# Loads of v behind the block moves, and a group's first sum and difference made with its last gate/value piece

## The chip, the cores and the metric

The kernel runs on one core of a Trainium2 chip. The metric is the device time of one execution in microseconds, the median of several runs. The engines named here are TensorE (PE in the profile; PEld is its weight load), VectorE (DVE), ScalarE (ACT), GpSimd (POOL) and SyncE (SP), which computes nothing and issues most of the DMAs. Each engine works through its own list of instructions in order; a semaphore wait of one instruction holds everything behind it on that engine.

## The reference

Two stages follow each other. The first is a linear attention with a decaying state, for 4 batches, 8 heads, 768 positions and head size 48; the second is a gated feed-forward block on the 3072 rows of 384 numbers that the first one leaves.

```python
# attention, for each position t
cur = einsum('bhd,bhe->bhde', u * k[t], v[t])
y[t] = einsum('bhd,bhde->bhe', r[t], state + cur)
state = w * state + einsum('bhd,bhe->bhde', k[t], v[t])
# feed-forward: x is (3072, 384), w_gate and w_val (384, 1536), w_out (1536, 384)
g = x @ w_gate
out = (g * sigmoid(g) * (x @ w_val)) @ w_out
```

## The kernel before

**Attention in blocks.** The 768 positions are cut in 6 chunks of 128, so there are 24 blocks (chunk times batch), numbered 0 to 23. For a block, r and k are scaled by powers of w (`scale_k` L329, `scale_r` L332, both on GpSimd), turned so that the head dimension lies on the partitions, multiplied into scores (L423), masked into `At` (L433, L437), and `outputs` (L476) multiplies `At` with v and the turned r with the state `Z`. `update` (L491, L503, L504) advances the state with k and v. `own_product` (L254, L255) and `own_sum` (L260) make the diagonal term with u.

**The turn of blocks 12 to 23** is made by sixteen small DMAs (`move_blocks`, L386, SyncE's queue), which move 32x32 blocks within `hats`, and two transposes on VectorE (`turn_blocks`, L401: first into `kT`, then into `rT`). Between these two transposes one piece of the feed-forward work is taken from the list of pieces. The moves of block s+1 overwrite what the transposes of block s read, so they wait for VectorE; they also wait for the scaled r and k. Two blocks share a buffer of scaled r, so the scaling of the r of an odd block (the even steps from 12 on, named `late`) waits for the moves of the even block before it.

**Loads.** `load` (L141) brings k and r of a block three steps ahead, `load_v` (L148) brings v one step ahead into one of four buffers; `outputs` and `update` of a block read v two steps after that. From block 12 on each is six DMAs. In the kernel before, step s of the main loop issues, in SyncE's queue: `load_v(s + 1)`, then (not when `late`) `load(s + 3)`, then the moves of s+1, then (when `late`) `load(s + 3)`.

**The feed-forward block** works on groups g of 256 rows (two attention blocks). From g = 2 on, two groups g and g+1 are taken together. Their gate and value products are made by `three_beside` (g = 2, 4, 6, beside the attention) and `three_units` (g = 8, 10, behind it): blocks of 3x3 are multiplied with 15 products instead of 18, from sums of weight blocks (`w_forms`, L700, GpSimd) and of x (L727); L770 are the products, L794 the additions that put them together in `hv`, L801 the sigmoid-gated unit, L794 also its multiplication. The additions, and the multiplication that gives `hT`, are mostly VectorE's; the last multiplication, of group g+1, is kept back in `last`.

**The output product** `project` (L589) uses 7 products instead of 8 on the halves of `hT` and of `w_out`. It needs sums and differences of the quarters of `hT`, which `h_sums` makes on VectorE: with n = 0 the sum L562 and the difference L563, with n = 1 L565 and L566. `two_projections` gives the order of the items "00 10 01 02 11 04 ...": the first digit j picks the group g or g+1, the second the product p. The item "10" starts with `h_sums(g, 0)`, and "02" is the first product that reads its result. The item "01" first does what `last` kept back, then `h_sums(g, 1)`.

**The order of the work** is written out by hand: pieces of the feed-forward block stand in one list, and `gaps` takes a share of them at five places of each step of the main loop. `queue` fills the list: for a pair the other items of the pair before, then the pieces of `three_beside`, then item "00" of this pair, then the last piece. Item "10" comes first when the next pair is queued. The tail behind the loop runs `three_units` and the rest of the projections.

Output stores (L613) go through ScalarE's queue. SyncE's DMAs and these share eight semaphores in turn, so that in the built program each DMA also waits for the one eight places before it.

Of the kernel before, what the change touches and what calls it, by code (L numbers as in the profile page):

```python
# [22 lines left out]
def fast(  # L23
# [102 lines left out]
    def places(i, n):  # L126

        if i < SWAPPED:
            return [(slice(0, P), slice(0, n), 0)]
        return [  # L130
            (slice(0, P), slice(0, n // 2), 0),
            (slice(0, 64), slice(n // 2, n), 64),
            (slice(64, P), slice(n // 2, n), -64),
        ]

    def load(i):
        c, b = divmod(i, B)
        for src, dst in zip((k, r), raw(i)):
            for p, h, o in places(i, H):
                rows = slice(P * c + p.start + o, P * c + p.stop + o)  # L140
                sp.dma_start(out=dst[p, h], in_=src[b, h, rows, :].rearrange("h t d -> t h d"))  # L141

    def load_v(i):
        c, b = divmod(i, B)
        for e in range(2):
            for p, a, o in places(i, HP):
                rows = slice(P * c + p.start + o, P * c + p.stop + o)
                sp.dma_start(  # L148
                    out=v_ld[i % 4][p, a, 64 * e : 64 * e + D],
                    in_=v[b, :, rows, :].rearrange("(a e) t d -> e t a d", e=2)[e][:, a],  # L150
                )
# [99 lines left out]
    def own_product(i):  # L251
        kl, rl = raw(i)
        rk = two.tile([P, H, D], FP32, name="rk", tag="rk")[:]
        pool.tensor_mul(rk, rl, kl)  # L254
        pool.tensor_mul(rk, rk, ub)  # L255
        rks[i] = rk

    def own_sum(i):
        dus[i] = three.tile([P, H], FP32, name="du", tag="du")
        dve.tensor_reduce(dus[i][:], rks.pop(i), axis=AX.X, op=ALU.add)  # L260
# [67 lines left out]
    def scale_k(i):  # L328
        pool.tensor_mul(khat[i % 4][:, :, 0:D], raw(i)[0], kscale)  # L329

    def scale_r(i):
        pool.tensor_mul(rhat_of(i)[:, :, 0:D], raw(i)[1], rscale)  # L332
# [32 lines left out]
    def turn(i):  # L365
        kr = khat[i % 4], rhat_of(i)
        tps = [next_psum(HP, P) for _ in kr]
        turned[i] = three.tile([P, HP, P], FP32, name="rT", tag="rT")
        for tp, t, dst, table in zip(tps, kr, (kT[i % 2], turned[i]), (pw[:, :, 1 : P + 1], pv)):
            for a in range(HP):  # L370
                pe.transpose(tp[:, a, :], pair(t, a), ident[:])  # L371
            if i < 4:
                dve.tensor_mul(dst[:], tp[:], table)
            else:
                act.copy(dst[:], tp[:])

    def move_blocks(i):


        h = hats[:].rearrange("p n h x -> p (n h x)")  # L380
        first, step = ((0, 1), (11, -1), (12, 1), (23, -1))[i % 4]
        for m in range(4):
            for q in range(4):
                src = h[32 * q : 32 * q + 32, P * first + 32 * m : P * first + 32 * m + 1]
                dst = h[32 * m : 32 * m + 32, P * 31 + 32 * q : P * 31 + 32 * q + 1]
                sp.dma_start(  # L386
                    out=bass.AP(
                        tensor=dst.tensor, offset=dst.offset,
                        ap=[list(dst.ap[0]), [-P, 2 * HP], [1, 32]],
                    ),  # L390
                    in_=bass.AP(
                        tensor=src.tensor, offset=src.offset,
                        ap=[list(src.ap[0]), [P * step, 2 * HP], [1, 32]],
                    ),
                )
# [152 lines left out]
    def h_quarters(g):  # L548
        return [
            hT[g][:, FH * k : FH * (k + 1), P * j : P * (j + 1)] for j in range(2) for k in range(2)  # L550
        ]

    def h_sums(g, n):
        h11, h12, h21, h22 = h_quarters(g)
        if g < THREES:
            t = three.tile([P, 2, FH, P], FP32, name="hs", tag="w_bits")
        else:
            t = room["hs"][2 * (g % 2) + n]
        x = part_of.setdefault(g, {})
        x["s"] = x.get("s", ()) + (t[:, 0], t[:, 1])  # L560
        if n == 0:
            dve.tensor_add(t[:, 0], h22, h21)  # L562
            dve.tensor_sub(t[:, 1], t[:, 0], h11)  # L563
        else:
            dve.tensor_sub(t[:, 0], h11, h21)  # L565
            dve.tensor_sub(t[:, 1], h12, x["s"][1])  # L566
# [62 lines left out]
    def two_projections(g):  # L629

        def item(j, p):
            if g >= FIRST and (j, p) == (0, 1):
                for do in wide.pop("last"):
                    do()
            if (j, p) in ((1, 0), (0, 1)):
                h_sums(g, p)
            elif (j, p) in ((1, 1), (0, 3)):
                h_sums(g + 1, p // 3)
            if g + 2 < N // 2:
                prepare_threes(g + 2, order.index(f"{j}{p}"))  # L640
            project(g + j, p)
        order = "00 10 01 02 11 04 03 12 05 06 13 14 15 16".split()
        return [lambda j=int(o[0]), p=int(o[1]): item(j, p) for o in order]


    FIRST, THREES = 2, 8
# [19 lines left out]
    wide, todo_forms, todo_x = {}, deque(), deque()  # L666
# [74 lines left out]
    def prepare_threes(g, n):  # L741
        if n == 6:
            x_forms(g)
        for _ in range(2):
            if todo_x:
                todo_x.popleft()()
        if g > THREES:
            return
        if n == 1:
            if g == FIRST:  # L750
                todo_forms.extend(in_place(0) + in_place(1))
            if g == THREES:
                todo_forms.extend(w_forms(g, 1))
        if n == 7:
            todo_forms.extendleft(reversed(w_forms(g, 0)))
        for _ in range(2):
            if todo_forms:
                todo_forms.popleft()()
# [26 lines left out]
    def three_beside(g):  # L785
# [18 lines left out]
        for t in range(4):  # L804
# [21 lines left out]
            for k in range(6):  # L826
                i, j = divmod(k, 2)
# [44 lines left out]
        steps, last = [], []  # L872
        for at, do in sorted(todo, key=lambda x: x[0]):
# [3 lines left out]
            if at == int(at):  # L877
                steps.append([])
            steps[-1].append(do)
        steps[-1].append(lambda: wide.update(last=last))  # L880
        pieces = [[] for _ in range(26)]
        for n, q in enumerate(steps):
            pieces[n if n < 3 else 3 + (n - 3) * 23 // 57] += q
# [140 lines left out]
    BLOCKS = 12  # L1024
# [85 lines left out]
    for s in range(4, N + 2):  # L1110
        if 4 < s < N:
            own_sum(s)
        late = BLOCKS < s + 1 < N and s % 2 == 0
        if s + 2 == SWAPPED:
            halves_of = two.tile([P, H, D], FP32, name="swapped", tag="rk")[:].rearrange(
                "p (n h) d -> p n h d", n=2
            )
            for p, o in ((slice(0, 64), 64), (slice(64, P), -64)):
                sp.dma_start(
                    out=halves_of[p], in_=scales[p.start + o : p.stop + o, 1:3, H // 2 : H]  # L1120
                )
        if s + 1 == SWAPPED:
            pool.tensor_copy(scales[:, 1:3, H // 2 : H], halves_of)
        if s + 1 < N:
            scale_k(s + 1)
            if not late:
                scale_r(s + 1)
            own_product(s + 1)
            load_v(s + 1)
            if s + 3 < N and not late:  # L1130
                load(s + 3)
        if s < BLOCKS:
            turn(s)
        gaps(s, 0)
        if 4 <= s - 1 < N:
            while small:
                small.popleft()()
            scores(s - 1)
            if s >= LATE:
                outputs(s - 2)  # L1140
                update(s - 2)
            gaps(s, 1)
        if BLOCKS <= s < N:
            turn_blocks(s)
        if late:
            scale_r(s + 1)
        if BLOCKS <= s + 1 < N:
            move_blocks(s + 1)
        if late and s + 3 < N:
            load(s + 3)  # L1150
        gaps(s, 2)
        if s - 2 >= 4 and (s < LATE or s > N):
            outputs(s - 2)
            update(s - 2)
        if s >= 5 and s % 2:
            queue((s - 3) // 2)
        if s < N:
            diagonal(s)
        if s - 2 >= 4:
            gaps(s, 3)  # L1160
        gaps(s, 4)
        if s == 12:

            dve.tensor_tensor(bad, held[:], wcol[:], ALU.not_equal)
            dve.tensor_reduce(badc, bad, axis=AX.X, op=ALU.add)
            dve.memset(ones, 1.0)
            n_ps = next_psum(HP, P)
            pe.matmul(n_ps[0:1, 0, 0:1], badc, ones, start=True, stop=True)
            act.copy(outside, n_ps[0:1, 0, 0:1])
# [426 lines left out]
```

## Time and profile before

| | |
|---|---|
| median of 3 runs | 600.33 us (599.98 to 602.51) |
| the profiled execution | 599.74 us |
| its span, first to last instruction | 598.0 us |
| granted TensorE clock, mean | 0.999 |
| busy: PE, DVE, ACT, POOL | 582.6, 405.0, 228.0, 313.6 us |
| block moves in SyncE's queue | 192 DMAs of 32 KB, median 2.0 us from issue to landing |
| loads of v, last twelve blocks | 24 DMAs of 48 KB and 48 of 24 KB, median 2.2 and 2.1 us |

In the rows of a timeline the first number is the start in microseconds from the span's beginning, the second the time from the first start to the last end of the instructions merged in the row, then come engine, line, operation, what is written and read, the shapes and the number of instructions. In square brackets stands for how long the engine was idle before the row and who released it. In the rows of the waits the three numbers are the total, the count and the longest, in microseconds. SPq is SyncE's queue: its rows last as long as the issue, and the transfer lands later.

### The profile page before, as it was taken

The numbers are of one execution on the slowest core, as the hardware profiler recorded it, in microseconds if no ns is written. First come the engines' busy times: TensorE is split into PE (matmuls) and PEld (weight loads), VectorE is DVE, ScalarE is ACT, GpSimd is POOL, SyncE is SP. The second block draws the span as 40 slices with busy tenths as digits, with TensorE's granted clock in tenths as the row PEclk, the third lists the DMA queues.
The fourth block names the chain that finished last, engine by engine and source line by source line (L and its number), as shares of the span: only waits on it lengthen the run. The fifth ranks groups of instructions, "written<-read, shape, count | busy, mean of one in ns | idle before, by whom it ended". The sixth has DMA issues, their size and how long they took to land.

```text
span 598.0 us, 12924 instructions
## 1 busy us (share of the span) xinstructions
PE 582.6 (97%) x5112; PEld 524.4 (88%) x5112; DVE 405.0 (68%) x682; ACT 228.0 (38%) x524; POOL 313.6 (52%) x352
## 2 busy tenths in 40 slices
PE   8799999999999999999999999899999999999996
PEld 7678888899888889988889988789988899988896
DVE  6877877369478877478778476769356685277650
ACT  3468887331353422254331344332034321233310
POOL 5789889998999402977610996503445100011000
PEclk9999999999999999999999999999999999999999
DMA  7989893232431323133233232300100000000001
GB/s 163 248 226 249 225 299 75 41 61 58 93 57 21 63 38 72 41 62 59 35 59 70 70 61 46 48 2 3 44 9 2 1 1 27 26 2 0 2 1 57
DMA packets 139830, 40.66 MB, mean 68 GB/s; under 512 B 130160, under 2 KB 133616, under 8 KB 139760
## 3 DMA queue, kind: packets, MB, share of 16 engines
q1 hardware_dynamic: 136304, 35.02, 27.3%
q10 hardware_dynamic: 3456, 4.72, 2.2%
q8 instruction: 42, 0.69, 0.5%
q14 instruction: 28, 0.23, 0.1%
HBM read 28.51 MB, written 4.72 MB: 56 GB/s over the span
## 4 chain that ended last, share of the span: by engine, by line
PE 83%; POOL 4%; DVE 3%; SPq 2%; issue 1%; DMA 1%; ACT 1%; POOLq 0%; DVEq 0%
PE bank L770 28%; PE bank L589 26%; PE ring L770 13%; PE bank L514 7%; PE ring L476 5%; PE ring L423 2%; SPq L386 2%; POOL wgv L242 1%; POOL s L700 1%; DVE hv L794 1%; PE ring L491 1%; PE ring L371 1%; DMA r_ld<-in_r_dram 1%; DVE hs L563 1%; POOL hats L332 0%
## 5 line engine op out<-in xcount | busy, mean ns | idle before, releaser
L794 DVE TENSOR_TENSOR hv<-hv,bank 128x512 f32<-128x512 f32 x132 | 88.0, 683 | 29.1 <-PE bank L770 18.7
L514 PE MATMUL bank<-xT,wgv 128*128 128x256 f32 x288 | 66.8, 385 | 0.6 <-ACT xT L480 0.6
L913 POOL TENSOR_TENSOR hv<-At,hats 128x512 f32<-128x512 f32 x8 | 10.2, 1272 | 107.0 <-ACT At L912 107.0
L770 PE MATMUL bank<-xf,wgv 128*128 128x256 f32 x256 | 66.0, 382 | 0.0
L350 ACT ACTIVATE At<-ident,du 128x128 f32<-128x128 f32 x176 | 60.5, 398 | 14.1 <-DVE hv L602 7.5
L794 ACT COPY hv<-bank 128x512 f32<-128x512 f32 x72 | 40.2, 586 | 61.3 <-PE bank L770 55.0
L514 PEld LDWEIGHTS bank<-xT,wgv 128*128 128x128 f32 x288 | 53.2, 190 | 8.9 <-ACT xT L480 0.9
L700 POOL TENSOR_TENSOR s<-wgv 128x256 f32<-128x256 f32 x39 | 30.0, 793 | 53.1 <-PE bank L589 53.0
L770 PEld LDWEIGHTS bank<-xf,wgv 128*128 128x128 f32 x256 | 47.8, 190 | 7.0 <-DVE kT L904 0.6
L589 PE MATMUL bank<-wo,hv 128*128 128x192 f32 x288 | 49.6, 327 | 0.0
L589 PEld LDWEIGHTS bank<-wo,hv 128*128 128x128 f32 x288 | 47.2, 190 | 0.6
L589 PE MATMUL bank<-wt,hs 128*128 128x192 f32 x240 | 42.1, 327 | 1.4 <-DVE hs L563 1.4
L595 ACT COPY hv<-bank 128x192 f32<-128x192 f32 x36 | 11.3, 318 | 83.9 <-PE bank L589 83.9
L589 PE MATMUL bank<-wo,hs 128*128 128x192 f32 x240 | 42.5, 327 | 0.0
L589 PEld LDWEIGHTS bank<-wt,hs 128*128 128x128 f32 x240 | 39.2, 190 | 2.4 <-issue 1.3
L589 PEld LDWEIGHTS bank<-wo,hs 128*128 128x128 f32 x240 | 39.5, 190 | 0.4 <-DVE hv L597 0.3
L801 ACT ACTIVATE hv<-hv 128x512 f32<-128x512 f32 (+1 forms) x33 | 21.1, 667 | 48.3 <-DVE hv L794 48.3
L770 PE MATMUL bank<-xT,s 128*128 128x256 f32 x152 | 35.5, 380 | 1.6 <-POOL s L700 1.6
L476 PE MATMUL ring<-At,v_ld 128*32 128x128 f32 x768 | 34.9, 273 | 1.5 <-DMA v_ld<-in_v_dram 1.5
L770 PE MATMUL bank<-xT,wgv 128*128 128x256 f32 x144 | 35.6, 380 | 0.0
L770 PEld LDWEIGHTS bank<-xT,s 128*128 128x128 f32 x152 | 28.6, 190 | 6.4 <-POOL s L700 2.0
L504 POOL TENSOR_TENSOR Z<-Z,w 48x192 f32<-48x192 f32 x32 | 17.3, 540 | 31.4 <-DVE Z L503 30.2
(190 smaller groups left out, 1296.2 us busy)
## 6 DMA issues: line engine op xcount, KB each, us to landing
hats<-hats SPq DMA_DIRECT2D x192, 32.0 KB, 2.0
w_bits<-in_moe_w_gate_dram SPq DMA_DIRECT2D x6, 768.0 KB, 6.1
w_bits<-in_moe_w_val_dram SPq DMA_DIRECT2D x6, 768.0 KB, 6.4
w_bits<-in_moe_w_out_dram SPq DMA_DIRECT2D x6, 768.0 KB, 7.0
out_dram<-hv ACTq DMA_DIRECT2D x24, 192.0 KB, 1.9
v_ld<-in_v_dram SPq DMA_DIRECT2D x24, 96.0 KB, 5.7
k_ld<-in_k_dram SPq DMA_DIRECT2D x8, 192.0 KB, 3.6
r_ld<-in_r_dram SPq DMA_DIRECT2D x8, 192.0 KB, 4.0
```

What stands on the lines that cost most here:

```text
L350: lambda h=h: act.activation(At[i % 2][:, h, :], ident[:], AF.Identity, scale=du[:, h : h + 1])
L386: sp.dma_start(out=bass.AP(tensor=dst.tensor, offset=dst.offset, ap=[list(dst.ap[0]), [-P, 2 * HP], [1, 32]],), in_=bass.AP(tensor=src.ten ...
L423: pe.matmul(ps[e][keys, a, cols], kT[i % 2][rows, at(i, a), keys], turned[i][rows, at(i, a), cols], start=True, stop=True, skip_group_chec ...
L476: pe.matmul(ps[32 * q : 32 * q + 32, cc, :], *x, start=start, stop=stop, skip_group_check=True,)
L504: pool.tensor_mul(ze, ze, w)
L514: pe.matmul(gv[:, o, :].rearrange("p (i t) -> p i t", i=2), wt[:, c, P * f : P * (f + 1)], xT[:, 2 * g % NX : 2 * g % NX + 2, c, :], start ...
L589: pe.matmul(ps, lhs[:, f, :], rhs[:, f, :], start=(f == 0 and n in (0, 1, 4)), stop=(f == FH - 1), skip_group_check=True,)
L595: act.copy({0: o1[:, 0:NH], 2: o1[:, NH:DM], 3: o2[:, NH:DM]}[n], ps)
L700: op(made[o], made[a], made[b])
L770: pe.matmul(ps[:, o], u[:, o], v, start=first and o == 0, stop=True, skip_group_check=True,)
L794: do(out, *(pair_of(wide[a][:]) if isinstance(a, str) else a for a in args))
L801: todo.append((at, lambda: act.activation(gate, gate, AF.Silu)))
```

## The change

Two edits. The first: for blocks 12 to 23 `load_v` is issued right behind the sixteen moves of the same block; for `late` steps that is still ahead of `load(s + 3)`. Blocks before 12 keep their order. The second: for the groups g = 2, 4 and 6 `h_sums(g, 0)` is no longer the first thing of item "10" of the projections but the last thing of the last piece of `three_beside`. For the others it stays where it was.

```diff
@@ two_projections / item
-            if (j, p) in ((1, 0), (0, 1)):
+            if (j, p) == (0, 1) or (j, p) == (1, 0) and not FIRST <= g < THREES:
                 h_sums(g, p)
             elif (j, p) in ((1, 1), (0, 3)):
                 h_sums(g + 1, p // 3)
@@ three_beside
-        steps[-1].append(lambda: wide.update(last=last))
+        steps[-1] += [lambda: wide.update(last=last), lambda: h_sums(g, 0)]
@@ main loop
             own_product(s + 1)
-            load_v(s + 1)
+            if s + 1 < BLOCKS:
+                load_v(s + 1)
             if s + 3 < N and not late:
                 load(s + 3)
...
         if BLOCKS <= s + 1 < N:
             move_blocks(s + 1)
+            load_v(s + 1)
         if late and s + 3 < N:
             load(s + 3)
```

(`FIRST` is 2, `THREES` is 8, `BLOCKS` is 12, `N` is 24.)

## The prediction

> **What bounds the kernel now.** I read the page first, then who waited for whom on TensorE, then the timelines around those waits, the SyncE queue last.
>
> ```profile
> PE 582.6 (97%) x5112; PEld 524.4 (88%) x5112; DVE 405.0 (68%) x682; ACT 228.0 (38%) x524; POOL 313.6 (52%) x352
> ```
>
> TensorE is busy for 582.6 of 598.0 us. No matmul is added or removed, so only its 15.4 us of idle time can change. By the busy time in stretches, 7.0 of them lie in the first 60 us and 5.4 at the end, where the change does nothing. Between 200 and 420 us TensorE waits four times, 3.0 us in all:
>
> ```profile
> PE bank L770 <- POOL s L700: 1.6, 1, 1.6
> PE bank L589 <- DVE hs L563: 1.4, 3, 0.6
> ```
>
> The second row is what the moved sum and difference (h_sums) feed: three groups, three waits. The first of them, by the timeline:
>
> ```profile
> 216.90 4.06 PE L589 MATMUL bank<-wo,hv 128*128 128x192 f32 x24
> 218.90 0.70 DVE L401 STREAM_TRANSPOSE kT<-hats 128x512 f32<-128x512 f32 x1
> 219.53 0.92 DVE L562 TENSOR_TENSOR hs<-hv 128x768 f32<-128x768 f32 x1
> 219.77 0.30 ACT L595 COPY hv<-bank 128x192 f32<-128x192 f32 x1
> 220.48 0.96 DVE L563 TENSOR_TENSOR hs<-hs,hv 128x768 f32<-128x768 f32 x1
> 221.59 2.19 PE L589 MATMUL bank<-wt,hs 128*128 128x192 f32 x12 [0.62 <-DVE hs L563]
> ```
>
> Only the transpose of kT (L401) stands between the gate/value work on VectorE and the sums. The second:
>
> ```profile
> 307.48 1.28 DVE L794 TENSOR_TENSOR hv<-hv,bank 128x512 f32<-128x512 f32 x2
> 309.61 4.17 PE L589 MATMUL bank<-wo,hv 128*128 128x192 f32 x24
> 310.26 0.74 DVE L437 COPY_PREDICATED At<-mask,ring 128x512 f32<-128x512 int32 x1 [1.50 <-ACT At L350]
> 310.88 0.73 DVE L503 TENSOR_TENSOR Z<-ring,Z 48x192 f32<-48x192 f32 x2
> 311.64 0.97 DVE L562 TENSOR_TENSOR hs<-hv 128x768 f32<-128x768 f32 x1
> 313.94 2.19 PE L589 MATMUL bank<-wt,hs 128*128 128x192 f32 x12 [0.16 <-DVE hs L563]
> ```
>
> VectorE idles 1.5 us in front of the masked copy L437, with the sums queued behind it. The third wait is at 407.68.
>
> The longest wait, at 377.38, is put down to GpSimd by the page. But the built program's waits show that these matmuls need a sum of a set finished at 364.4, and VectorE's addition of the bank. That addition is the first of the three at 376.59; with 0.69 us each it ends at 377.28. It stood behind a transpose that waited for block moves:
>
> ```profile
> 374.48 0.71 DVE L401 STREAM_TRANSPOSE kT<-hats 128x512 f32<-128x512 f32 x1 [1.95 <-DMA hats<-hats]
> 376.59 1.84 DVE L794 TENSOR_TENSOR hv<-hv,bank 128x512 f32<-128x512 f32 x3
> 377.38 1.97 PE L770 MATMUL bank<-xT,s 128*128 128x256 f32 x8 [1.64 <-POOL s L700]
> ```
>
> The block moves' queue, SyncE's:
>
> ```profile
> 340.46 11.71 SPq L386 DMA_DIRECT2D hats<-hats  x16
> ...
> 352.21 1.96 SPq L141 DMA_DIRECT2D k_ld<-in_k_dram  x3
> 354.21 1.90 SPq L141 DMA_DIRECT2D r_ld<-in_r_dram  x3
> 356.22 3.88 SPq L148 DMA_DIRECT2D v_ld<-in_v_dram  x6
> 360.20 12.50 SPq L386 DMA_DIRECT2D hats<-hats  x16
> ```
>
> Write M22 for the moves of block 22, v22 for its load of v, L23 for the loads of k and r. From 340.46 to 372.70 the queue issues without a pause, and the last of M22 lands at 374.1: SyncE's issue time does reach TensorE here, once.
>
> **First part: the sums earlier.** The built order of VectorE differs in two places alone.
> Group 2 (219 us): L562 and L563 go in front of the kT transpose, which delays them from 218.90 to 219.53. They come 0.63 us earlier. Can TensorE use it? 12 matmuls of this kind take 1.95 us (0.1625 each), so the 24 from 216.90 would be followed at 220.80; the sums now release at 221.59-0.63 = 220.96. Still a short wait, so the gain is 0.63. ScalarE's copy of the same bank (L595), which the matmul also needs, ended at 220.07. The kT transpose comes 1.9 us later; its reader is a later score. rT, which releases the next moves, has the same four instructions ahead of it as before: nothing.
> Group 4 (308 us): they go in front of L437 and the two L503, and can start at 308.76, where the pair of L794 ends, in time that VectorE now idles. They end near 310.7 (0.95 each, no GpSimd work beside them then). TensorE's natural place is 309.61+24x0.1625 = 313.51, so the gain is 313.94-313.51 = 0.43, with 2.8 us of cover left; ScalarE's copy of the bank is at 311.87 to 312.19, so it does not bind. L437 slips from 310.26 to about 310.7 and the two L503 with it, some 0.4; behind them wait GpSimd's scaling of Z, which is then idle till 328.19, and outputs that TensorE starts at 330.8. Nothing.
> Group 6: the built order is the same as before (both transposes already stand in front), so its 0.57 us stays.
> Sum: 0.63+0.43 = 1.06 us.
>
> **Second part: the loads of v.** Six DMAs (3.9 to 4.9 us of issue) per block, blocks 12 to 23, move behind the sixteen moves. The queue's end was v20, L22, M20, v21, M21, L23, v22, M22, v23, M23; it becomes L22, M20, v20, M21, v21, L23, M22, v22, M23, v23. So between two runs of moves there is still exactly one load of v, an earlier block's. M21 to M22: before L23 and v22 (3.96+3.98), after v21 and L23. M22 starts at 360.2 both times. VectorE's rT would have let it go at 357.7, but the 2.5 us aren't gained. At the first run, M12, v12 does go away, but L14 in front was held by GpSimd till 118.74 with SyncE idle from 113.7: nothing.
> What does move: L15, L17, L19, L21, L23 are issued 4 us later. The first four are read 7 us or more after they would land (L15: issued till 162.1, read at 174.2). L23 is tight: it would be issued 356.2 to 360.1, and rows of its kind land after 2.5 to 2.9 us, so r is there at about 362.1, where GpSimd's product L254 starts at 361.28 now: 0.8 us late. Behind it stand L255 and one sum of weights, read by TensorE at about 378; GpSimd then has 2.3 us idle in front of 366.73. Hidden.
> v itself comes some 16 to 27 us later: v22 is issued at 372.8 and read at 416.5. Its buffer's readers are two blocks back and done; SyncE's waits on them cost nothing.
> The output stores on ScalarE's queue share semaphores with SyncE's DMAs, each waiting for the one eight back. In the new program two wait for later moves of M20 (the second until about 328.6, where it is issued at 328.48: 0.1 us, on an engine 38% busy), and eight wait for the last moves and v23, landed by 394, the first being due at 422.
> M22 now follows L23 and not v22. The Trainium skill (DMA: Bandwidth & Descriptors, "Queues, rings and completion order") says that each DMA engine consumes descriptors in ring order, which speaks against the change, as L23 moves 384 KB against v22's 192. The rows: k and r land after 2.6 to 2.9 us, v after 2.1. By the rule M22's first moves land up to 0.8 us late; its last is issued 12 us later, when that backlog is gone, so by the rows it lands as now. I take 0; 0.8 stays for the range.
>
> **Does the 1.06 survive to the end?** The stall at 377 closes a loop: TensorE's last L589 (327.9) releases GpSimd at 328.19, which works without a gap till the scaling of r ends at 340.44; that releases M21, then v21, L23, M22, VectorE, TensorE. Its start moves with TensorE, so the stall arrives as much earlier and stays as long. From 416 on TensorE waits for no one. So the profiled execution of 599.74 us (span 598.0) becomes 598.7; the median of the runs, 600.33, lies 0.6 above it and becomes **599.3**.
>
> **Rivals.**
> *The load's move frees M22.* If an issue of v really leaves the stretch M21 to M22, M22 starts 2.4 us earlier and the stall (377.38-375.57 = 1.8) goes: 597.5. For it: the queue has no pause there. Against: the count above.
> *The sums don't reach TensorE*, because something else releases those matmuls: 600.3. Against: the 0.14 us from the end of L563 to the matmul, both times.
> *Slower: M22 lands later.* The loop has no slack at 377, so each us by which its SyncE stretch grows is one on TensorE. M22 already takes 12.50 where M23 takes 10.49; its slow issues (1.26 and 1.54 us against 0.61) coincide with 16 KB packets of the instruction queue at 361.5 and 368.9. Two more such meetings cost 1.9: 601.2. From 1.06 us on this outweighs the gain, and a whole load of v too much in the stretch (4.0) would give 603.3.
>
> **How the numbers follow.** Likeliest 0.68 (598.5 to 600.3: the sums give from 0.63, group 2 alone, to 1.22, both waits wholly gone, with the 0.6 us to either side by which the profiled run and the median differ); freed 0.09; no effect 0.09; slower 0.14. I take half a per cent, 3.0 us, as about what a measurement of this kernel can tell from no change. Below 597.3: half of the freed case and a trace of the likeliest, 0.06. Above 603.3: half of the slower case, 0.07. The rest, 0.87, is within. The range leaves out most of the freed case and the worse half of the slower one: 597.9 to 601.4.
>
> **What the new profile would show.** Right: the waits of L589 for hs gone at group 4 and at about 0.2 in group 2, still 0.6 in group 6; VectorE with both sums before L437 near 308.7; one load of v between every two runs of moves; a wait of 1.6 to 2 us on L770 near 376; L254 of block 23 waiting for r. Wrong: that last wait on L770 gone or doubled, a new wait of TensorE on At or Z, or ScalarE held before a store.

## The result, and the profile after

The changed kernel takes 598.58 us in the median of 22 runs (597.7 to 601.37), the kernel before, run beside it on the same chip, 599.95 us (598.75 to 602.51). That is 1.37 us less in the medians; the ratio is 0.9979, with a 95% interval of 0.9970 to 0.9987, or 0.8 to 1.8 us. The profiled executions give 596.9 against 598.0 us of span, and 598.61 against 599.74 us in all. TensorE has the same work as before; this row of the page is that of after:

```profile
PE 582.5 (98%) x5112; PEld 524.6 (88%) x5112; DVE 404.6 (68%) x682; ACT 228.3 (38%) x524; POOL 313.2 (52%) x352
```

The waits of TensorE between 200 and 420 us, after (total, count, longest, in us):

```profile
PE bank L770 <- POOL s L700: 1.2, 1, 1.2
PE bank L589 <- DVE hs L563: 0.6, 1, 0.6
```

Of the three waits on hs (1.4 us in all) one is left, the one of group 6. The wait on L770 is there still, 0.4 us shorter. Now the timelines of after, all engines, at group 2:

```profile
217.32 4.06 PE L589 MATMUL bank<-wo,hv 128*128 128x192 f32 x24
219.32 0.95 DVE L562 TENSOR_TENSOR hs<-hv 128x768 f32<-128x768 f32 x1
220.31 0.96 DVE L563 TENSOR_TENSOR hs<-hs,hv 128x768 f32<-128x768 f32 x1
221.18 0.70 DVE L401 STREAM_TRANSPOSE kT<-hats 128x512 f32<-128x512 f32 x1
...
221.41 2.19 PE L589 MATMUL bank<-wt,hs 128*128 128x192 f32 x12
```

The transpose stands behind the sums. From the first of the 24 matmuls to the first on hs it is 4.09 us, before 4.69. At group 4:

```profile
308.62 0.95 DVE L562 TENSOR_TENSOR hs<-hv 128x768 f32<-128x768 f32 x1
309.55 4.17 PE L589 MATMUL bank<-wo,hv 128*128 128x192 f32 x24
309.61 0.96 DVE L563 TENSOR_TENSOR hs<-hs,hv 128x768 f32<-128x768 f32 x1
310.48 0.73 DVE L437 COPY_PREDICATED At<-mask,ring 128x512 f32<-128x512 int32 x1
...
313.56 2.11 PE L589 MATMUL bank<-wt,hs 128*128 128x192 f32 x12
```

The sums fill the time in which VectorE had idled in front of L437, and are done 3 us before TensorE reads them. The end of SyncE's queue, after:

```profile
339.78 11.13 SPq L386 DMA_DIRECT2D hats<-hats  x16
351.00 3.95 SPq L148 DMA_DIRECT2D v_ld<-in_v_dram  x6
355.00 1.89 SPq L141 DMA_DIRECT2D k_ld<-in_k_dram  x3
356.93 1.90 SPq L141 DMA_DIRECT2D r_ld<-in_r_dram  x3
358.94 12.67 SPq L386 DMA_DIRECT2D hats<-hats  x16
371.72 3.95 SPq L148 DMA_DIRECT2D v_ld<-in_v_dram  x6
```

Between M21 (339.78) and M22 (358.94) there is one load of v, ahead of L23 now instead of behind it, and the queue has no pause. What follows from it on VectorE and TensorE, after:

```profile
373.36 0.71 DVE L401 STREAM_TRANSPOSE kT<-hats 128x512 f32<-128x512 f32 x1 [1.51 <-DMA hats<-hats]
...
375.48 1.84 DVE L794 TENSOR_TENSOR hv<-hv,bank 128x512 f32<-128x512 f32 x3
...
376.27 1.97 PE L770 MATMUL bank<-xT,s 128*128 128x256 f32 x8 [1.22 <-POOL s L700]
```

It is the same chain as before, from the moves' landing to the transpose, the addition and the matmul. (The sum of GpSimd, to which the row puts the wait down, ends within 0.1 us of that addition and is held by the same landing, so the trace alone doesn't tell the two apart; that it is the addition rests on the waits of the built program.)

**Where the time went.** All kernels here give TensorE the same matmuls in the same order, so the start of each can be set against that of the same matmul before. The difference changes in a few places only, given here by the times of the kernel before. In the changed kernel it is +0.42 us from 60 us on (a slower start, where nothing was changed). It falls by 0.59 at 221.6 us (group 2), of which 0.10 is lost again at 225.7, by 0.40 at 313.9 and 0.22 at 318.0 (group 4), and by 0.42 at 377.4. The sums gave 1.12 us of this, and the 0.42 at 377.4 makes up for the slower start: 1.1 us, as the two spans have it.

### The profile page after: what moved, and what is told of

Its sections match the earlier page's. It is cut to its first block, busy times and chain, and to the rows that moved or that the text cites. A ratio compares the mean times of both kernels' runs of the same rounds, so it can differ in the third digit from the quotient of the medians.

```text
span 596.9 us, 12929 instructions
## 1 busy us (share of the span) xinstructions
PE 582.5 (98%) x5112; PEld 524.6 (88%) x5112; DVE 404.6 (68%) x682; ACT 228.3 (38%) x524; POOL 313.2 (52%) x352
## 4 chain that ended last, share of the span: by engine, by line
PE 85%; POOL 4%; SPq 2%; DVE 1%; issue 1%; DMA 1%; ACT 1%; POOLq 0%
PE bank L770 28%; PE bank L589 27%; PE ring L770 13%; PE bank L514 7%; PE ring L476 5%; PE ring L423 3%; SPq L386 2%; POOL wgv L242 1%; PE ring L491 1%; PE ring L371 1%; POOL hats L332 1%; POOL rk L254 0%; POOL hats L329 0%; POOL rk L255 0%; DMA k_ld<-in_k_dram 0%
## 5 line engine op out<-in xcount | busy, mean ns | idle before, releaser
L794 DVE TENSOR_TENSOR hv<-hv,bank 128x512 f32<-128x512 f32 x132 | 88.0, 684 | 28.9 <-PE bank L770 18.5
L770 PE MATMUL bank<-xf,wgv 128*128 128x256 f32 x256 | 66.0, 382 | 0.0
L794 ACT COPY hv<-bank 128x512 f32<-128x512 f32 x72 | 40.2, 586 | 60.8 <-PE bank L770 54.5
L770 PEld LDWEIGHTS bank<-xf,wgv 128*128 128x128 f32 x256 | 47.8, 190 | 7.0 <-DVE kT L904 0.6
L770 PE MATMUL bank<-xT,s 128*128 128x256 f32 x152 | 35.5, 380 | 1.2 <-POOL s L700 1.2
L770 PE MATMUL bank<-xT,wgv 128*128 128x256 f32 x144 | 35.6, 380 | 0.0
L770 PEld LDWEIGHTS bank<-xT,s 128*128 128x128 f32 x152 | 28.6, 190 | 5.9 <-POOL s L700 1.6
```

Of the source, the lines that this page charges most:

```text
L770: pe.matmul(ps[:, o], u[:, o], v, start=first and o == 0, stop=True, skip_group_check=True,)
L794: do(out, *(pair_of(wide[a][:]) if isinstance(a, str) else a for a in args))
```

## The experiments

Each kernel's time stands beside that of the kernel before on the same chip, since the chips differ; in brackets is the number of executions.

**The sums alone.** Against before:

```diff
-            if (j, p) in ((1, 0), (0, 1)):
+            if (j, p) == (0, 1) or (j, p) == (1, 0) and not FIRST <= g < THREES:
...
-        steps[-1].append(lambda: wide.update(last=last))
+        steps[-1] += [lambda: wide.update(last=last), lambda: h_sums(g, 0)]
```

> Only the second edit: the sums earlier, the loads of v where they were before. Theory A (the sums give the gain, the loads of v nothing): the waits of L589 for hs at groups 2 and 4 shrink as in the changed kernel, M22 starts some 0.7 us before 360.2, and the time is 0.9 to 1.1 us below the kernel before, about 598.9 to 599.1. Rival B (the loads of v give it): within 0.3 us of the kernel before. Rival C (half from each): 0.6 us below.

598.13 us (12 runs) against 599.09 (23): 0.96 less in the medians, ratio 0.9990 (0.9977 to 1.0003). The interval takes in no change; the trace is clearer. TensorE's difference to before falls at the sums as in the changed kernel, in all by 1.12 us, and by 0.54 at 377. M22 starts at 358.30, 1.9 us before 360.20 and not 0.7: M21 took 11.22 us instead of 11.71, and the start of the kernel was 0.3 us faster too. So theory A holds for the sums, and the stall at 377 moves in a way that it doesn't explain.

**The loads alone.** Against before:

```diff
-            load_v(s + 1)
+            if s + 1 < BLOCKS:
+                load_v(s + 1)
...
             move_blocks(s + 1)
+            load_v(s + 1)
```

> Only the first edit: loads of v behind the moves, the sums where they were before. Theory A: the stretch from M21 to M22 still holds one load of v and L23, so M22 starts within 0.6 us of 360.2, TensorE's wait on L770 near 377 stays between 1.2 and 2 us, and the time is that of the kernel before to 0.4 us. Rival B: 1.0 to 1.4 us below the kernel before. Rival D (the later L23 or v costs something that the sums hid): 0.5 us or more above it.

598.21 us (12) against 599.09 (23): 0.88 less, ratio 0.9983 (0.9973 to 0.9994). More than theory A allows. The difference to before falls in one place, at 377.4, by 1.16 us: the wait on L770 is 0.48 us and not 1.64. M22 starts at 359.72, within 0.6 of 360.20 as A has it, but its sixteen issues take 11.98 us and not 12.50.

**The other two orders.** The changed kernel has the loads of v of odd and even blocks behind the moves. In the first of these two the odd blocks' are ahead, in the second the even blocks':

```diff
@@ odd_before
-            if s + 1 < BLOCKS:
+            if s + 1 < BLOCKS or late:
                 load_v(s + 1)
...
             move_blocks(s + 1)
-            load_v(s + 1)
+            if not late:
+                load_v(s + 1)
```

```diff
@@ even_before
-            if s + 1 < BLOCKS:
+            if s + 1 < BLOCKS or not late:
                 load_v(s + 1)
...
             move_blocks(s + 1)
-            load_v(s + 1)
+            if late:
+                load_v(s + 1)
```

> The changed kernel, but the loads of v of the odd blocks from 13 on are ahead of their moves again; those of the even blocks stay behind. The queue's end is M20, v20, v21, M21, L23, M22, v22, v23, M23: no load of v between M21 and M22. Theory A (one load of v in that stretch is what M22 waits for): M22 starts when VectorE's rT lets it, near 357.2 and not 358.94, the kT transpose comes at about 371.9 and not 373.36, the wait of 1.2 us on L770 goes, and the time is 1.2 us below the changed kernel, about 597.4. Rival E (the stall comes from GpSimd, to which the profile puts it down, or from the moves' own landing): the wait stays and the time is the changed kernel's to 0.3 us.

> The changed kernel, but the loads of v of the even blocks are ahead of their moves again; those of the odd blocks stay behind. The queue's end is v20, M20, M21, v21, L23, v22, M22, M23, v23: two loads of v between M21 and M22. Theory A (the stretch has no slack): M22 starts 4.0 us later, near 362.9, the wait on L770 grows from 1.2 to about 5.2 us, and the time is 4.0 us above the changed kernel, about 602.6. Rival F (some of it is taken up, for TensorE has other pieces to do or the moves go faster without a load behind them): 1 to 3 us above. Rival E: the changed kernel's to 0.3 us.

**odd_before**: 596.32 us (6) against 599.09 (23), ratio 0.9949 (0.9934 to 0.9964), the fastest kernel of this study. Its queue, with the moment it idles in front of M22:

```profile
350.46 1.96 SPq L141 DMA_DIRECT2D k_ld<-in_k_dram  x3
352.47 1.90 SPq L141 DMA_DIRECT2D r_ld<-in_r_dram  x3
356.75 12.44 SPq L386 DMA_DIRECT2D hats<-hats  x16
369.31 7.93 SPq L148 DMA_DIRECT2D v_ld<-in_v_dram  x12
```

and the place of the stall on VectorE and TensorE:

```profile
371.42 0.69 DVE L401 STREAM_TRANSPOSE kT<-hats 128x512 f32<-128x512 f32 x1
...
373.69 2.75 PE L770 MATMUL bank<-xT,s 128*128 128x256 f32 x12
```

SyncE is done with L23 at 354.4 and waits 2.4 us for VectorE's rT. The transpose no longer waits for the moves, and the twelve matmuls, which had been 4 and 8 with the stall between them, run through. Rival E, by which the wait stays, falls.

**even_before**: 605.23 us (6) against 599.09 (23), ratio 1.0091 (1.0069 to 1.0114). M22 starts at 364.48, 24.36 us behind M21 instead of 19.16, and the stall grows to 4.46 us. That is 3.2 us more than after, less than the 4.0 of theory A; but the time is 6.1 us above before. The rest is in the clock. The row of the stall in this kernel's timeline, and then its stretches around the stall, with the granted TensorE clock ahead of the last two figures:

```profile
380.14 3.75 PE L770 MATMUL bank<-xT,s 128*128 128x256 f32 x8 [4.46 <-POOL s L700]
```

```profile
374.00:378.00 4.00, 1.68 (x8) 1.14 (x6) 0.75 (x2) 0.05 (x1) 0.75 (x1) 1.00 0.22 33
378.00:380.00 2.00, 0.00 (x0) 0.00 (x0) 2.00 (x4) 0.00 (x0) 2.00 (x3) 0.86 0.00 0
380.00:386.00 6.00, 5.86 (x14) 4.73 (x15) 2.77 (x5) 1.96 (x4) 2.21 (x4) 0.50 0.28 44
386.00:388.00 2.00, 2.00 (x11) 1.70 (x10) 1.33 (x3) 0.00 (x0) 0.00 (x0) 0.93 0.31 51
388.00:394.00 6.00, 6.00 (x29) 5.30 (x28) 4.52 (x8) 2.80 (x7) 3.34 (x4) 1.00 0.31 51
```

(In each row the stretch and its length come first, then the busy time of PE, PEld, DVE, ACT and POOL, then the clock.) For 6 us and a little more TensorE runs at half speed: eight matmuls take 3.75 us, which in the changed kernel took 1.97. Behind the stall the difference to before rises from 2.76 to 5.77 us over the next 3 us of work, so 3.0 us are lost to the clock, as much again as the stall itself grew by. The span is 6.9 us longer than that of the changed kernel: 3.2 of stall, 3.0 of clock, 0.4 at 295 us, in an earlier stretch of the same kind, and 0.3 at 364 us. The Trainium skill (TensorE: Matmul & The Clock Gate, "Part 1: The HAM clock gate") says that the clock goes to half after an idle window of about 3.4 us, with windows that run freely, and comes back after a busy one. The trace agrees: 0.50 behind a stall of 4.46 us, and 1.00 behind the 1.22 of the changed kernel.

**A shorter stall on purpose, and the changed kernel once more.** half_load has three of the six DMAs of v22 ahead of M22, against the changed kernel:

```diff
-    def load_v(i):
+    def load_v(i, parts=(0, 1)):
...
-        for e in range(2):
+        for e in parts:
...
+            elif s + 1 == 22:
+                load_v(22, (0,))
...
-            load_v(s + 1)
+            load_v(s + 1, (1,) if s + 1 == 22 else (0, 1))
```

> The changed kernel, but three of the six DMAs of v22 are ahead of M22, three behind. M22 starts 1.98 us later (three issues of 0.66), so the wait on L770 grows from 1.2 to about 3.2 us. Theory A (each us in the stretch is one on TensorE, and a wait of 3.2 us costs no more than itself): 2.0 us above the changed kernel, and the granted clock stays 1.00 behind the wait. Rival K (a wait of this length already lowers TensorE's clock, as the one of 4.46 us did, with 0.50 for some 6.8 us, 3.4 us lost): 5.4 us above.

> The changed kernel once more, to see how much of a profile's detail repeats. If the details are fixed by the program: the wait on L770 near 376 is 1.2 us to 0.1, the run of moves M22 takes 12.7 us, the sums shift TensorE by 0.67 us at group 2 and 0.41 at group 4, and the time is 1.0 to 1.8 us below the kernel before. If the stall near 376 hangs on where slow issues fall in one execution: the sums' shifts repeat to 0.1 us and the wait on L770 differs by 0.3 us or more.

The changed kernel takes 598.86 us (12) against 600.25 (34) here, ratio 0.9981 (0.9970 to 0.9991), as the first time. Its shifts at the sums repeat: 0.60, 0.40 and 0.22 us (then 0.59, 0.40, 0.22). The wait on L770 is 1.35 (then 1.22), but M22 starts at 360.41 and not 358.94 behind the same start of M21, and is issued in 11.49 us and not 12.67.

half_load takes 601.02 us (12), 2.16 above it; the expectation of 2.0 is met, but not by its reason. In its profile the wait is only 2.06 us, 0.7 more and not 2.0, another 0.5 us is lost at 363 us, and the clock behind the wait is 1.00; that execution took 599.24. Four more took 599.35 to 599.52; the other seven 600.94 to 602.39, with a mean granted clock of 0.994 to 0.997 instead of 0.998 to 1.000. Losing 0.003 of 598 us is 1.8 us; the medians of the two groups lie 1.9 apart, and one window of 3.4 us at half clock (the length from the page above) would by estimate cost 1.7. Where in the execution they lost it is not shown: none of them was profiled, and 12 of the 34 executions of the kernel before and 4 of the 12 of the changed kernel have a mean clock of 0.994 to 0.997 too. So the 5.4 us of rival K don't come, and whether a stall of 2 to 3 us costs some executions their clock stays open.

**The loads of the last four blocks alone**, to see whether the 0.48 us of the loads alone come from M21 to M22, or from earlier blocks. Against before:

```diff
-            load_v(s + 1)
+            if s + 1 < 20:
+                load_v(s + 1)
...
             move_blocks(s + 1)
+            if s + 1 >= 20:
+                load_v(s + 1)
```

> The kernel before, with the loads of v of blocks 20 to 23 alone behind their moves; blocks 12 to 19 and the sums are as before. Theory G (having L23 and not v22 right in front of M22 makes M22 land earlier, whichever execution): the wait on L770 near 377 is 0.5 us as with all twelve loads moved, not 1.6, and the time is 0.7 to 1.1 us below the kernel before. Theory H (the 0.5 was the luck of one execution, or came from blocks 12 to 19): the wait is 1.0 us or more and the time is the kernel before's to 0.4 us.

599.23 us (12) against 600.25 (34), 1.02 less, ratio 0.9986 (0.9974 to 0.9999), and a wait on L770 of 0.89 us. The time is what theory G expects, the wait lies between the two, and one profile of the kernel before decides nothing. So there are two more of it, and one more of the loads alone:

> The kernel before, a second profile. Theory G (the order L23, v22 in front of M22 is what makes the stall long): the wait on L770 near 377 is again 1.5 us or more, longer than in any profile of a kernel with the loads of v behind the moves and the sums late (0.5 and 0.9). Theory H (its length is set by how three packets of the instruction queue meet the moves in that execution): it differs from 1.64 by 0.3 us or more, and the times at which 16 KB packets start between 345 and 372 us fit the slow issues.

> The kernel before, a third profile, with the same expectations as the second.

> Only the loads of v behind the moves, a second profile. Theory G: the wait on L770 near 377 is 0.9 us or less again. Theory H: it lies anywhere from 0.4 to 1.7 us.

The same program, the kernel before, waits 0.51 us in its second profile and 1.67 in its third:

```profile
376.08 1.97 PE L770 MATMUL bank<-xT,s 128*128 128x256 f32 x8 [0.51 <-POOL s L700]
```

```profile
377.09 1.97 PE L770 MATMUL bank<-xT,s 128*128 128x256 f32 x8 [1.67 <-POOL s L700]
```

What differs are the slow issues in SyncE's queue. From the first issue of M21 to the last of M22 every profile has three issues (in two kernels four) of 0.8 to 1.9 us instead of 0.6, and within 0.6 us of three of them a packet of 16 KB of the instruction queue (q8) starts; the fourth meets an instruction packet of 8 KB. Over all thirteen profiles, between 250 and 400 us, 129 of the 2321 issues for k, r, v and the moves are slow (over 0.78 us), and 125 of these have the start of a 16 KB packet within 0.52 us; only 3 of the 128 packets that fall among issues have no slow one. That the packet holds the issue up is inferred from this; no run changed the packets. The slow pair of issues in the first profile of before, in a window of its own, and what the instruction queue moved in 0.15 us of it:

```profile
360.90 1.94 SPq L386 DMA_DIRECT2D hats<-hats  x2
```

```profile
q8 instruction: 1, 0.02, 39.0%
```

For each profile but odd_before's, where M22 waits for VectorE, in us: from the first issue of M21 to the last landing of M22; the slow issues, and what they have over 0.63, the usual time; the difference; and the wait on L770 near 377. (The 0.10 of loads_only_2 is below what the view of the waits lists. In that profile 0.65 us had been lost at 364, as told below, and came off the stall.)

| kernel | M21 to landing | slow issues | over 0.63 | rest | wait |
|---|---|---|---|---|---|
| before | 33.63 | 1.81, 1.26, 1.54 | 2.72 | 30.91 | 1.64 |
| before_2 | 32.51 | 1.18, 1.39, 1.05 | 1.73 | 30.78 | 0.51 |
| before_3 | 33.64 | 1.83, 1.33, 1.48 | 2.75 | 30.89 | 1.67 |
| sums_only | 33.10 | 0.98, 0.96, 1.46, 1.39 | 2.27 | 30.83 | 1.10 |
| loads_only | 32.71 | 1.45, 1.30, 1.14 | 2.00 | 30.71 | 0.48 |
| loads_only_2 | 32.91 | 1.60, 0.88, 1.61 | 2.20 | 30.71 | 0.10 |
| loads_late | 33.04 | 1.87, 0.90, 1.46 | 2.34 | 30.70 | 0.89 |
| changed | 33.36 | 1.26, 1.51, 1.62 | 2.50 | 30.86 | 1.22 |
| changed_again | 33.49 | 1.72, 1.61, 1.34 | 2.78 | 30.71 | 1.35 |
| half_load | 34.83 | 1.23, 1.11, 1.41, 0.84 | 2.07 | 32.76 | 2.06 |
| even_before | 36.74 | 1.76, 1.36, 0.83 | 2.06 | 34.68 | 4.46 |

The rest is constant to 0.2 us where the queue has one load of v in the stretch, with v22 behind L23 or v21 ahead of it; it is 2.0 us more with half a load and 3.9 more with a whole one. So theory H holds for the profiles: with the same issues in the stretch, the landing of M22 follows the slow issues, and the stall spans 1.2 us in one and the same program. Theory G would have 0.1 us at most (30.85 in the mean of the four with the old order, 30.74 of the five with the new). What stays open: the two kernels with only loads moved were 0.88 and 1.02 us faster in the median than before, each time with an interval that leaves out zero, while their profiles give a reason for 0.1 us. The clock isn't the reason: among the executions with a mean clock of 0.998 or more alone the medians differ by 0.88 and 0.86 us. Whether the packets meet the new order more kindly on the average, so few profiles can't tell: 2.40 us over 0.63 in the three of before, 2.18 in the three with only loads moved, 2.36 in all five with the loads behind.

**The sums still earlier**, on top of odd_before: ahead of the two additions of L794 that come before them.

```diff
+        todo.append((45 + 13.95, lambda: h_sums(g, 0)))
         steps, last = [], []
...
-        steps[-1] += [lambda: wide.update(last=last), lambda: h_sums(g, 0)]
+        steps[-1].append(lambda: wide.update(last=last))
```

> The kernel with the loads of v of odd blocks ahead of the moves and of even blocks behind, and in the last piece the first sum and difference now stand ahead of the two additions of banks that precede them in the changed kernel (1.27 us of VectorE). Theory A: the last wait on hs, 0.57 us at group 6, goes, and what is left of group 2's; 0.6 us below the kernel with that order of loads alone, 0.3 to 0.9. Rival L (the two additions come 2.3 us later, their bank is free later and TensorE or the last multiplication waits for it): no gain, or up to 2 us above it, with a new wait of L589 for L794.

597.99 us (11) against 600.25 (34), ratio 0.9965 (0.9955 to 0.9975), where odd_before has 0.9949; so there is no gain. The waits of this kernel between 60 and 420 us, and the new one at group 6:

```profile
PE bank L589 <- DVE hv L597: 1.1, 3, 0.8
```

```profile
409.81 2.22 PE L589 MATMUL bank<-wo,hs 128*128 128x192 f32 x12 [0.76 <-DVE hv L597]
```

No wait on hs is left; at group 6 TensorE gains 0.69 us where the wait was and loses 1.10 us three to four microseconds later. At groups 2 and 4, by the same L597, 0.57 of the 1.12 us is left. Theory A is right on the wait that goes. Rival L is right on the sum, with L597 in the place of L794: the last multiplication on VectorE waits 0.91 us for ScalarE behind the delayed additions, L565, L566 and L597 come later, and the next matmul of hs waits for L597.

## Why the prediction was right, and where it was not

The prediction gave 599.3 us, 1.06 below the 600.33 of the first three runs, and 598.7 for the profiled execution. Measured were 1.37 us less (0.8 to 1.8), and 598.61 for that execution. By its steps:

- **Group 2, 0.63.** Right: 0.59, and 0.59 to 0.60 in all six profiles with this edit in this form. The sum left out that 0.10 of it goes again four microseconds later, where the next weight load on hs starts right behind VectorE's L597. The short wait that should remain is there: 4.09 us for the 24 matmuls that need 3.90.
- **Group 4, 0.43.** Right: 0.40 at this place in all six. Another 0.22 us came four microseconds later, and the prediction didn't have it: it looked at the waits of PE and missed this row of PEld, of the kernel before. The weight load of the next matmuls on hs waits for an addition on VectorE that stands behind the sums:

```profile
318.04 1.92 PEld L589 LDWEIGHTS bank<-wo,hs 128*128 128x128 f32 x12 [0.26 <-DVE hv L597]
```

 So the sums gave 1.12 us where 1.06 were predicted. That the total is so near is in part luck, as the 0.10 lost and the 0.22 gained were in no step.
- **Group 6, nothing.** Right: 0.57 us both times.
- **The queue still holds one load of v between M21 and M22, so the move of the loads is worth nothing.** The count is right, and odd_before and even_before show that it is this count that decides. By the profiles the step is right to 0.1 us; by the medians of the two kernels with loads alone it may be 0.9 us short, and that is open. The 0.8 us that a queue in ring order might have cost, with L23 right ahead of the moves, don't show: the rest of the table is no longer with L23 there.
- **The start of the stall at 377 moves with TensorE and its length stays.** The loop is as described; that its length stays was wrong. One profile's 1.64 us were taken for a property of the program, where the same program has 0.51 to 1.67. So the 0.42 us that the changed kernel gained there in its profile is within what the packets do. Its start lost 0.42 us too, and by this luck the two spans differ by what the sums alone give.
- **L254 of block 23 waits 0.8 us for r, hidden.** Not in the first profile: r landed at 360.53 and L254 ran at 360.69, as the queue was there 1.3 us before the predicted 360.1. But of the seven profiles with this load behind v21 the other six have the wait, from 0.22 to 1.30 us, the longest in the second profile of the changed kernel. It isn't wholly hidden: in four of them (loads_only, loads_only_2, half_load, even_before) VectorE's addition that runs beside the delayed L254 takes 0.92 to 1.47 us instead of 0.7 and ends 0.55 us behind it, and TensorE is 0.1 to 0.65 us later at 364, by a path over VectorE that the prediction didn't look at. In loads_only_2:

```profile
361.21 1.00 POOL L254 TENSOR_TENSOR rk<-r_ld,k_ld 128x384 f32<-128x384 f32 x1 [0.80 <-DMA r_ld<-in_r_dram]
361.29 1.47 DVE L794 TENSOR_TENSOR hv<-hv 128x512 f32<-128x512 f32 x1
...
363.87 1.99 PE L770 MATMUL bank<-xT,wgv 128*128 128x256 f32 x8 [0.39 <-DVE hv L794]
```

 It costs little in the end, since the matmul at 377 waits for the queue all the same.
- **The rival "the load's move frees M22", 597.5,** had its price right: odd_before, which does free it, lies 2.77 us below before, the rival 2.83.
- **The rival "slower", 603.3 for a whole load too much,** had the right mechanism and too low a price: even_before lies 6.1 us above before and not 3.0, as the stall is long enough to halve the clock for 6 us behind it.

## What to carry to other kernels

Count the issues between the two ends of a loop that has no slack: moving a load behind its run of moves does not shorten the loop as long as another block's load takes its place, and moving the loads of every second block instead of all doubled the gain. Before a stall of a microsecond or two is costed from one profile, the same program should be profiled again, and single matmuls compared rather than spans. A longer wait can cost more than its length: the one of 4.46 us lost another 3.0 us to the clock.

## What the runs showed of the hardware

- An issue of SyncE that coincides with a 16 KB packet of the instruction queue takes 0.8 to 1.9 us instead of 0.6. Within one stretch of 33 us that is 1.7 to 2.8 us, and it differs by a microsecond between executions of one program. The Trainium skill (Runtime: NRT & Kernel Launch, "Instruction fetch mechanics") tells that a sequencer fetches its instructions in blocks of 16 KiB over a DMA queue of its own, and calls the cost mostly hidden. Here the slow issues that go with such packets are not hidden, as they lie on the queue that TensorE waits for.
- A stall of 4.46 us was followed by some 6 us of TensorE at half the granted clock; stalls of 0.1 to 2.1 us were followed by none in the profiles.
- An addition of VectorE (hv<-hv, 128x512) took 0.92 to 1.47 us beside GpSimd's L254 and 0.7 us without it.
- Where the profile lists the wait on L770 near 377 it puts it down to GpSimd's sum. The runs that changed only SyncE's queue removed and lengthened it.
